# Moving the dummy matmuls at the start of a GEGLU kernel, and storing its last row tile in one piece

## The chip, the cores and the metric

One core of a Trainium2 chip runs the whole kernel. The metric is the device time of one execution in microseconds. A time is quoted as the median of several executions, with the lowest and highest. The profile of a kernel is one execution, recorded by the hardware; its span is about 1.8 us shorter than the device time.

## The reference, cut to what matters

```python
B, S, Dm, Df = 1, 2048, 1024, 3584            # x, w_gate, w_up, w_down in bf16
g = jnp.einsum("bsd,df->bsf", x, w_gate)
u = jnp.einsum("bsd,df->bsf", x, w_up)
h = jax.nn.gelu(g, approximate=True) * u
return jnp.einsum("bsf,fd->bsd", h, w_down)
```

## The kernel before

The matmuls of this kernel take `x` transposed, so its first 512 rows are transposed before the first of them. They come as four row tiles of 128 rows. Each is loaded, transposed by eight TensorE transposes into one PSUM bank, and copied to SBUF; row tile 1 is copied by ACT, the others by VectorE. In the profile TensorE starts a transpose every 0.107 us at first and every 0.056 us later, so its clock begins at about half rate; dummy matmuls on a constant tile ("dummies") run ahead of the transposes and between them, to bring the full clock sooner. In the profiles PE is TensorE, PEld its weight loads, DVE VectorE, ACT ScalarE; SPq and ACTq are the queues on which the sync engine and ACT issue loads and stores. A transfer lands when the profile shows it complete.

```python
def load_x(c):
    for i in range(NS):                                   # four row tiles, all on the sync queue
        nc.sync.dma_start(out=xn, in_=x2[r0 : r0 + P, :])

def turn(xT, xn, c, i):
    for ko in range(NKB):
        nc.tensor.transpose(tp[:, ko, :], xn[i][:, ko * P : (ko + 1) * P], ident)
    # ... the last tile's copy is cut in two
    (on_act if i == 1 else on_dve)(out=xT[c][:, ks, i * P : (i + 1) * P], in_=tp[:, ks])

# ...
keep_warm(NWARM, N)                                       # NWARM = 6 dummies of 512 columns
for i in range(NS):
    if i in (1, 2):
        keep_warm(5 - 2 * i, 2 * P)                       # 3, then 1 dummies of 256 columns
    turn(xT, xn0, 0, i)
plain(bank[0:4], 0, range(0, 2), parts=2)                 # first computing matmuls
```

`plain` begins with matmuls on the first 256 rows only (row tiles 0 and 1). Its first two matmuls need the first weights of `w_gate`, its third and fourth those of `w_up`; the ninth is the first that needs row tiles 2 and 3. At the end of the kernel the last row tile of the output leaves in two halves, on two queues:

```python
r0, h = (2 * ip + 1) * N + i * P, N // 2
for n, queue in enumerate((nc.sync, nc.scalar)):
    st = slot([P, h], bf16, "st")
    nc.scalar.copy(out=st, in_=e[i][:, n * h : (n + 1) * h])
    queue.dma_start(out=out2[r0 : r0 + P, n * h : (n + 1) * h], in_=st)
```

## Time and profile before

| | kernel before |
|---|---|
| time, median of 3 | 540.51 us (540.12 to 540.99) |
| span of the profiled run | 538.4 us |
| TensorE busy | 534.3 us, 99% |
| first and third computing matmul start | 7.23 and 7.45 us |
| end of the last matmul to the end of the span | 3.21 us |

Read the table from below: what is not TensorE's unbroken work is 7.2 us at the start and 3.2 us at the end, and the change is about those two stretches alone.

### The profile page before, as it was taken

To read this page: it belongs to the slowest core of one execution; us is meant where nothing else is said; L and a number is where in the kernel's file an instruction comes from. 1 tells how busy PE (TensorE), PEld (TensorE's weight loads), DVE (VectorE), ACT (ScalarE), POOL (GpSimd) and SP (SyncE) were. 2 spreads that over 40 slices of the span, in tenths; PEclk is the share of its full clock that TensorE was granted. 3 is DMA by queue.
4 is the path that set the end of the run, shared out by engine and by line. 5 is a ranking of instruction groups with operands and counts; after the bars stand their busy time and mean duration, and the time that the engine had idled before them with its cause. 6 is when DMAs were issued, how large, how long until landed. Compare 5 with 4: busy or idle time off the path is not lost.

```text
span 538.4 us, 7452 instructions
## 1 busy us (share of the span) xinstructions
PE 534.3 (99%) x2410; PEld 382.1 (71%) x2410; DVE 341.7 (63%) x524; ACT 261.4 (49%) x464; POOL 238.2 (44%) x215
## 2 busy tenths in 40 slices
PE   9999999999999999999999999999999999999997
PEld 5568686767767646888867677676868685488886
DVE  2986766767676895684955455555554649676730
ACT  2556675666666410255355555555555551114431
POOL 1079966777773500000097767676766600000000
PEclk9999999999999999999999999999999999999999
DMA  9765666749472999989872223241420049473751
GB/s 249 173 165 174 179 183 169 226 127 270 126 230 80 384 384 306 287 175 303 231 195 79 78 80 92 66 134 48 132 72 8 2 162 389 171 236 96 234 185 50
DMA packets 108326, 93.29 MB, mean 173 GB/s; under 512 B 17280, under 2 KB 93184, under 8 KB 108288
## 3 DMA queue, kind: packets, MB, share of 16 engines
q1 hardware_dynamic: 108144, 92.75, 59.2%
q8 instruction: 19, 0.31, 0.2%
q14 instruction: 19, 0.16, 0.1%
q10 hardware_dynamic: 144, 0.07, 0.0%
HBM read 74.45 MB, written 15.20 MB: 167 GB/s over the span
## 4 chain that ended last, share of the span: by engine, by line
PE 99%; DMA 1%; ACT 0%; issue 0%
PE bank L111 98%; PE bank L454 1%; DMA xn<-in_x_dram 1%; PE bank L509 0%; ACT st L418 0%
## 5 line engine op out<-in xcount | busy, mean ns | idle before, releaser
L93 POOL TENSOR_TENSOR s<-w 128x512 fp32r<-128x512 bf16 x102 | 119.1, 1190 | 162.8 <-PE bank L111 113.7
L111 PE MATMUL bank<-t,s 128*128 128x512 f32 x648 | 151.7, 390 | 0.0
L111 PEld LDWEIGHTS bank<-t,s 128*128 128x128 f32 x648 | 121.7, 188 | 25.5
L111 PE MATMUL bank<-xT,w 128*128 128x512 bf16 (+1 forms) x504 | 109.5, 376 | 0.0
L107 ACT COPY p<-bank 128x512 f32<-128x512 f32 x124 | 69.9, 590 | 45.3 <-PE bank L111 44.9
L111 PEld LDWEIGHTS <-w 128*128 128x128 bf16 x504 | 48.2, 98 | 57.8 <-issue 3.4
L90 DVE TENSOR_TENSOR hT<-g,bank 128x512 bf16<-128x512 f32 x112 | 76.8, 687 | 17.7 <-PE bank L111 4.5
L90 DVE TENSOR_TENSOR sum<-bank,p 128x512 f32<-128x512 f32 x54 | 37.3, 690 | 79.7 <-PE bank L111 78.6
L179 ACT ACTIVATE g<-sum 128x512 f32<-128x512 f32 x81 | 51.4, 635 | 74.6 <-DVE sum L90 74.3
L111 PE MATMUL bank<-q 128*128 128x512 f32 x240 | 59.0, 389 | 0.0
L93 POOL TENSOR_TENSOR s<-w,s 128x512 fp32r<-128x512 bf16 x50 | 57.8, 1179 | 0.0
L93 POOL TENSOR_TENSOR s<-s,w 128x512 fp32r<-128x512 f32 x50 | 57.3, 1168 | 0.0
L111 PE MATMUL bank<-t,sa 128*128 128x512 f32 x216 | 55.9, 401 | 0.0
L111 PE MATMUL bank<-tb,s 128*128 128x512 f32 x216 | 53.3, 389 | 0.0
L107 ACT COPY u<-bank 128x512 f32<-128x512 f32 x62 | 35.5, 589 | 33.5 <-PE bank L111 33.3
L111 PEld LDWEIGHTS bank<-q 128*128 128x128 f32 x240 | 45.1, 188 | 9.3
L111 PE MATMUL bank<-raw,hT 128*128 128x512 bf16 x224 | 48.7, 379 | 0.0
L102 ACT CAST tb<-raw 128x512 fp32r<-128x512 bf16 x28 | 17.3, 626 | 62.0 <-PE bank L111 26.7
L111 PEld LDWEIGHTS bank<-t,sa 128*128 128x128 f32 x216 | 40.6, 188 | 9.4
L111 PEld LDWEIGHTS bank<-tb,s 128*128 128x128 f32 x216 | 40.6, 188 | 8.4
L90 DVE TENSOR_TENSOR bank<-bank,p 128x512 f32<-128x512 f32 x54 | 37.7, 699 | 8.7 <-PE bank L111 6.2
L90 DVE TENSOR_TENSOR q<-hT 128x512 fp32r<-128x512 bf16 x56 | 38.4, 686 | 4.8 <-PE bank L111 4.8
(45 smaller groups left out, 443.8 us busy)
## 6 DMA issues: line engine op xcount, KB each, us to landing
raw<-in_w_down_dram SPq DMA_DIRECT2D x77, 256.0 KB, 5.1
q<-td SPq DMA_DIRECT2D x60, 256.0 KB, 5.2
w<-in_w_gate_dram SPq DMA_DIRECT2D x27, 512.0 KB, 5.9
w<-in_w_up_dram SPq DMA_DIRECT2D x27, 512.0 KB, 6.6
td<-m SPq DMA_DIRECT2D x12, 768.0 KB, 4.5
w<-td SPq DMA_DIRECT2D x6, 1024.0 KB, 9.5
out_dram<-st SPq DMA_DIRECT2D x31, 128.0 KB, 1.7
td<-w SPq DMA_DIRECT2D x2, 768.0 KB, 6.4
```

The lines of the kernel that those rows point to most:

```text
L90: nc.vector.tensor_tensor(out=out, in0=a, in1=b, op=op)
L93: nc.gpsimd.tensor_tensor(out=out, in0=a, in1=b, op=op)
L102: nc.scalar.copy(out=t, in_=src)
L107: nc.scalar.copy(out=t, in_=ps)
L111: nc.tensor.matmul(ps, lhsT=lhs, rhs=rhs, start=start, stop=stop, skip_group_check=True)
L179: nc.scalar.activation(g, src, ACT.Gelu_apprx_tanh)
L454: nc.tensor.transpose(tp[:, ko, :], xn[i][:, ko * P : (ko + 1) * P], ident)
```

## The change

Its intent: close the idle gap ahead of the first transpose with a seventh dummy, take away the dummies that delay row tile 1, and replace two small copies and two stores at the very end by one of each. A third edit drops an exception, so that in the last pass one more `w_down` tile is fetched as two halves.

```diff
-    NWARM = 6
+    NWARM = 7
...
-        for kh in (range(2),) if j < NJ - (1 if last else 2) else (range(1), range(1, 2)):
+        for kh in (range(2),) if j < NJ - 2 else (range(1), range(1, 2)):
...
         def put21(i):
-            if not last or i < NS - 1:
-                store(ip, 1, i, 0, lambda st: nc.scalar.copy(out=st, in_=e[i]))
-                return
-            r0, h = (2 * ip + 1) * N + i * P, N // 2
-            ...  (two copies, two stores, as above)
+            store(ip, 1, i, 0, lambda st: nc.scalar.copy(out=st, in_=e[i]))
...
-            if i in (1, 2):
-                keep_warm(5 - 2 * i, 2 * P)
+            if i == 2:
+                keep_warm(2, 2 * P)
```

## The prediction

> **What bounds the kernel now.** I read the page first (busy shares and the chain of waits by engine), then that chain in order of time, then the timeline of the first eight and the last seven microseconds, because the diff touches nothing else.
>
> ```profile
> PE 534.3 (99%) x2410; PEld 382.1 (71%) x2410; DVE 341.7 (63%) x524; ACT 261.4 (49%) x464; POOL 238.2 (44%) x215
> ...
> PE 99%; DMA 1%; ACT 0%; issue 0%
> ```
>
> TensorE is the bound over the whole span of 538.4 us; nothing else holds more than 1% of the chain. So a change can only gain where TensorE does not yet work, or does work that is not needed. The chain in order of time (start, length, what) shows where that is:
>
> ```profile
> 0.74 2.77 DMA xn<-in_x_dram
> 3.51 0.05 issue
> 3.56 1.04 PE bank L454 x8
> 4.59 0.64 PE bank L509 x3
> 5.24 0.85 PE bank L454 x8
> 6.09 0.21 PE bank L509
> 6.30 1.09 PE bank L454 x16
> 7.39 527.79 PE bank L111 x2368
> 535.18 0.02 issue
> 535.21 0.03 ACT st L418
> 535.23 0.24 issue
> 535.48 0.38 ACT st L418
> ```
>
> L454 are the transposes of the four row tiles, L509 the dummies between them, L111 every matmul that computes. The 2368 matmuls are one uninterrupted piece of 527.79 us that the diff does not enter. What can change is the 7.4 us ahead of it and the 3.2 us behind it (535.18 to 538.4). The timeline of the start:
>
> ```profile
> 2.01 0.15 PEld L509 LDWEIGHTS <-const-bfloat16-1.0 128*128 128x128 bf16 x1 [0.28 <-issue]
> 2.44 0.15 PEld L509 LDWEIGHTS <-const-bfloat16-1.0 128*128 128x128 bf16 x1 [0.28 <-issue]
> 3.56 0.77 PEld L454 LDWEIGHTS <-xn 128*128 128x128 bf16 x8 [0.97 <-DMA xn<-in_x_dram]
> 6.12 1.01 ACT L457 COPY xT<-bank 128x1024 bf16<-128x1024 bf16 x1 [4.11 <-PE bank L454]
> 7.23 17.45 PE L111 MATMUL bank<-xT,w 128*128 128x256 bf16 x88
> ```
>
> The weight loads of two dummies start 0.43 us apart, so a 512-column dummy takes 0.427 us. The sixth starts at 2.86 (timeline) and hands TensorE on at 2.86 + 0.43 = 3.29; the first transpose starts only at 3.56, when row tile 0 has landed. That **hole of 0.27 us** is the only idle time of TensorE at the start. The end:
>
> ```profile
> 532.04 0.58 ACT L413 CAST st<-bank 128x512 bf16<-128x512 f32 x1 [2.59 <-PE bank L111]
> 532.65 0.33 SPq L363 DMA_DIRECT2D out_dram<-st  x1
> 535.21 0.65 ACT L418 CAST st<-bank 128x256 bf16<-128x256 f32 x2 [2.59 <-PE bank L111]
> 535.61 0.33 SPq L419 DMA_DIRECT2D out_dram<-st  x1
> 535.89 0.37 ACTq L419 DMA_DIRECT2D out_dram<-st  x1
> ```
>
> The first two lines are the third row tile in one copy and one store, the form that the change gives to the last one; the other three are the last tile in halves.
>
> **What the Trainium skill says.** (1) TensorE: Matmul & The Clock Gate, Part 1: the array starts at half clock and goes to full after a window of about 3.4 us of activity; the window is free-running, so the moment varies by some 500 ns from run to run; a matmul of N columns issues every N/1.2 ns before and N/2.4 + 2.5 ns after. The trace agrees: 0.427 us for 512 columns early; transposes last 314 ns at first and 219 ns later. From 6.09 to 7.23 there are 16 transpose starts; n at 0.107 and 16 - n at 0.056 us make 1.14 for n near 5, so the full clock came at about 6.6 us. (2) The same page, Part 4, says that transposes do not count as activity in the same way. Here the clock came after 3.0 us that held 24 or more transposes and only 0.85 us of dummies, so the trace rather speaks against it; in any case both kernels issue the same dummy columns. (3) DMA: Bandwidth & Descriptors, "Anatomy of one DMA", puts most of the cost of a small transfer on a fixed receipt. That page describes another issuing path, but the trace agrees: a store of 128 KB lands 1.7 us after issue, those of 64 KB after 1.6 (sync queue) and 1.7 (ACT's queue). (4) ScalarE: Activation LUTs, "What ACT_TABLE_LOAD costs": 186 ns + 0.833 ns per column for one instruction without pointer operands. The trace's copies are a little shorter: 585 ns for 512 columns, 376 for 256.
>
> **The change part by part.** *Start.* Dummy columns before: 6x512 + 3x256 + 1x256 = 4096. After: 7x512 + 2x256 = 4096. Nothing is saved in work; dummies are moved into the hole. The landings, taken from the DMA view one issue at a time: the row tiles are issued at 0.74, 1.19, 1.65 and 2.12 and land after 2.8, 3.0, 3.8 and 4.2 us, thus at 3.5, 4.2, 5.4 and 6.3; the first weights of gate and up are issued at 2.59 and 3.07 and land after 4.2 and 4.1, thus at 6.8 and 7.2.
>
> With these landings and the clock at 6.6 as before, the changed start runs so: the seventh dummy ends at 2.86 + 2 x 0.427 = 3.71 (tile 0 is there since 3.5); tile 0 until 3.71 + 8 x 0.107 = 4.57 (tile 1 since 4.2); tile 1 until 5.42; two dummies of 0.213 until 5.85 (tile 2 since 5.4); then seven transposes at half clock until 6.60 and nine at 0.056 until 7.10 (tile 3, first needed at 6.65, since 6.3). The first real matmul starts at 7.10 instead of 7.23: **0.13 us earlier**. The check: 0.27 us of idle time at half clock is worth 0.135 us at full clock. The ACT copy of tile 1, which that matmul needs and which ended at 7.13, only just in time, now starts near 5.65 and ends near 6.7: that tight place is relieved. The up weights (7.2) are first needed by the third matmul at 7.10 + 0.22 = 7.32: still in time.
>
> *End.* Now: last matmul done 535.18; copies from 535.21 to 535.86; the second store is issued on ACT's queue at 535.89 and lands 1.67 later at 537.55, and 0.84 us of closing follow. After: one copy 535.21 + 0.585 = 535.79, store issued 0.03 later (535.82, as on the third tile: 532.62 to 532.65), lands 1.70 later at 537.52. **About 0.03 us earlier**, a tie: one copy is 0.07 us shorter than the overlapped pair, and the sync queue's 128 KB store is about 0.03 slower than the 64 KB store on ACT's.
>
> *A third thing in the diff:* in the last pass one more w_down tile, the last but one, is fetched as two halves. Its load is issued at 500.75 and lands at 504.33; VectorE's subtraction of it starts at 504.98, so the second half may come 0.6 us later without being felt. An issue takes 0.4 us. Cost: 0.
>
> *Sum:* 0.13 + 0.03 = 0.16 us for a run whose clock came at 6.6, out of 540.5: 0.03%.
>
> **The rivals.** *The start is bound by landings, not by TensorE.* If the clock is granted two microseconds earlier, both kernels wait for tiles 2 and 3 (5.4, 6.3) and for the up weights (7.2), and the start gains nothing. Taking the clock's moment as evenly spread over one window (0.78 + 3.4 to 7.6, an estimate from the skill's window and the first dummy), about two fifths of the runs have no gain, the rest 0.1 to 0.16: mean 0.08, so about 540.4. *The tighter arrivals cost:* the slack of tiles 1 to 3 falls from 0.85, 0.65, 0.5 to 0.4, 0.4, 0.35 us; row tiles landing 0.5 us later than in this trace would make tile 1 wait. Each 0.1 us beyond the slack costs 0.05 to 0.1; unlikely, since nothing moves the loads. *The closed hole changes when the clock comes:* an unbroken stretch may qualify a window that one with a hole misses. That would save half of a window at most, and the landings cut it to 0.5 us or so, in some runs only. *The split fetch stalls TensorE near 505 us:* VectorE is close behind there (three operations of 0.60 for each 1.81 us of TensorE), so a late half would show at once; the slack of 0.6 us speaks against it. Any of these stays below 0.6 us, a tenth of a per cent. A change of 2%, 10.8 us, would need a broken 527.79 us piece, and the order of instructions on all engines beyond start and end is the same.
>
> **Range and chances.** Mean start gain 0.08 to 0.13 and end gain 0.03 from 540.51: 540.51 - 0.15 = 540.36, say 540.35. The spread of the runs before (540.12 to 540.99, 0.87 us) is about what a wandering clock can do: a clock 1 us later costs 0.5 us. The range must hold that spread for a median of a few runs: 539.85 to 540.9. Faster by 2%: 0.003; slower by 2%: 0.003.
>
> **What would show it.** In the profile after: seven dummies 0.43 apart, then transposes with no wait for row tile 0 (before: 0.97 on the weight-load row) and none for tiles 1 to 3; the piece of real matmuls about 0.13 earlier, if the clock's step from 314 to 219 ns transposes is again near 6.6; one 0.58 us copy and one store of 1.7 us at the end; the long piece unchanged at 527.8. Wrong would be: a new wait for a row tile, a clock step in another window, a hole near 505 us, or a 128 KB store that lands later than 1.75 us after its issue.

## The result, and the profile after

| | before | after |
|---|---|---|
| time, median of 6 | 540.32 us (539.98 to 540.99) | 540.26 us (539.66 to 540.87) |
| span of the profiled run | 538.4 us | 538.8 us |
| first computing matmul | 7.23 us | 7.49 us |
| third computing matmul | 7.45 us | 7.91 us |
| end of the last matmul to the last landing | 2.38 us | 2.34 us |

The ratio is 0.9999, with a 95% interval of 0.9986 to 1.0012: no difference that can be seen. So the time is as predicted, but the one profile of the changed kernel is 0.4 us longer than that of the kernel before, against a predicted 0.16 us shorter. That needs an explanation. Its page first:

```profile
PE 534.1 (99%) x2409; PEld 381.2 (71%) x2409; DVE 341.5 (63%) x524; ACT 261.4 (49%) x463; POOL 238.5 (44%) x215
...
PE 98%; DMA 1%; SPq 0%; ACT 0%; issue 0%
```

One point of the chain's share has gone from TensorE to other things. The chain of waits in order of time (start, length, what) tells which; line numbers are 7 lower than before in this part of the kernel, so L447 are the transposes and L412 the last copy:

```profile
...
2.12 4.87 DMA xn<-in_x_dram
6.99 0.05 issue
7.04 0.62 PE bank L447 x8
7.66 0.22 PE bank L111 x2
7.88 0.03 issue
7.91 527.77 PE bank L111 x2366
535.68 0.02 issue
535.71 0.58 ACT st L412
```

The chain no longer runs back through TensorE's dummies but through a load: row tile 3, issued at 2.12, took 4.87 us to land. Then the chain holds the transposes of that tile, two matmuls, and a wait. The timeline of the start shows the same from TensorE's side; the bracket at the end of a line is idle time before it and what ended it:

```profile
0.78 3.15 PE L502 MATMUL bank<-const-bfloat16-1.0 128*128 128x512 bf16 x7 [0.78 <-PEq L640]
...
5.46 1.01 ACT L450 COPY xT<-bank 128x1024 bf16<-128x1024 bf16 x1 [3.45 <-PE bank L447]
...
6.30 0.45 PEld L447 LDWEIGHTS <-xn 128*128 128x128 bf16 x8 [0.94 <-DMA xn<-in_x_dram]
...
7.03 0.45 PEld L447 LDWEIGHTS <-xn 128*128 128x128 bf16 x8 [0.28 <-DMA xn<-in_x_dram]
...
7.91 1.10 PEld L111 LDWEIGHTS <-w 128*128 128x128 bf16 x11 [0.31 <-DMA w<-in_w_up_dram]
```

The seven dummies run without a gap into the transposes, as intended. But TensorE then waits three times: for row tile 2, for row tile 3, and for the first weights of `w_up`. None of these waits is in the kernel before's profile. The loads are issued at the same times in both (0.74, 1.19, 1.66, 2.12; up weights 3.07), yet row tile 2 landed at 6.26 instead of 5.45, tile 3 at 6.99 instead of 6.31, and the up weights at 7.87 instead of 7.17. The transposes also change from long to short at about 5.0 us, so the clock stepped up 1.6 us earlier than in the first profile. (The clock that the profile gives as granted reads 1.00 throughout; the step is read from these durations.) Everything behind the start is unchanged: the difference in start time between the two kernels' 2368 computing matmuls is 0.46 us at the third, 0.50 at the 200th and 0.50 at the last.

At the end, the DMA view of the changed kernel's last store (size, us from issue to landing):

```profile
out_dram<-st SPq DMA_DIRECT2D x1, 128.0 KB, 1.7
```

One copy of 0.58 us and one store that lands 1.7 us later: that half of the prediction is as written.

### The profile page after: what moved, and what is told of

Its sections match the earlier page's. It is cut to its first block, busy times and chain, and to the rows that moved or that the text cites. A ratio compares the mean times of both kernels' runs of the same rounds, so it can differ in the third digit from the quotient of the medians.

```text
span 538.8 us, 7447 instructions
## 1 busy us (share of the span) xinstructions
PE 534.1 (99%) x2409; PEld 381.2 (71%) x2409; DVE 341.5 (63%) x524; ACT 261.4 (49%) x463; POOL 238.5 (44%) x215
## 4 chain that ended last, share of the span: by engine, by line
PE 98%; DMA 1%; SPq 0%; ACT 0%; issue 0%
PE bank L111 98%; DMA xn<-in_x_dram 1%; SPq L440 0%; PE bank L447 0%; ACT st L412 0%
```

## The experiments

**Two theories.** *Clock theory*: the start is TensorE's own work at half clock, as the prediction's main sum has it, and the first profile after was an unlucky one. *Landing theory*: the start waits for loads in most runs, so moving dummies can gain nothing there. The noise came first, with the kernel before against itself, the changed kernel again, and each half of the change alone.

**aa_before** (no edit), timed in 5 rounds:

> The kernel before, unchanged, as the measure of noise and a second look at its start. Both theories: ratio to itself 1.000, with an interval of about 0.1% either way, so that a gain of 0.1 to 0.16 us (0.03%) cannot be read from the time. Landing theory (the start is set by when row tiles 2 and 3 and the first up weights land, in most runs): the third computing matmul starts within 0.1 us of the latest of the landings, and that moment differs from the first profile's 7.45 us by some tenths of a us because the landings differ. Clock theory (the start is set by TensorE's own work at half clock): it starts at 7.45 plus half of the shift of the clock's step from 6.6 us.

Measured: 540.16 us (539.88 to 540.25), the kernel before beside it 540.38 (539.91 to 540.75, 9 runs), ratio 0.9996 with an interval of 0.9982 to 1.0009. So a kernel differs from itself by as much as the change was to gain. The profile brought something that neither theory had. Its chain in order of time:

```profile
...
5.30 0.72 PE bank L454 x8
6.02 0.02 issue
6.04 1.02 ACT xT L457
7.06 0.04 issue
7.11 527.95 PE bank L111 x2368
```

The clock stepped at about 5.7 us here, TensorE was done with its transposes before 6.9, the up weights had landed at 6.98, and the first matmul waited for **ACT's copy of row tile 1**, which ended at 7.05. There is a third thing that can hold the start, and both expectations missed: the third matmul came at 7.32, against 7.08 at the latest by landings (6.98 + 0.1) and 7.0 by the clock.

**after_again** (the changed kernel, no edit), 5 rounds:

> The changed kernel again. Landing theory: same time as before within the noise, and in its profile a wait of TensorE for a row tile or for the first weights whenever the clock's step comes before about 5.8 us. Clock theory: a clock step near or after 6.6 us and no wait for a landing, with the third computing matmul about 0.13 us earlier than the kernel before would have it. Both: seven dummies, no wait for row tile 0; end of the last matmul to landing of the last store about 2.34 us (2.38 before).

Measured: 540.17 us (539.50 to 540.69), ratio 0.9996, interval 0.9983 to 1.0008: the same as aa_before had against itself. Its profile is again bound by landings although the clock stepped at about 5.8: row tile 2 at 6.29, up weights at 7.91, third matmul at 7.96. Last matmul to last landing: 2.34 us.

**start_only** and **end_only**: one half of the change each.

```diff
 # start_only, from the kernel before
-    NWARM = 6
+    NWARM = 7
-            if i in (1, 2):
-                keep_warm(5 - 2 * i, 2 * P)
+            if i == 2:
+                keep_warm(2, 2 * P)
```

```diff
 # end_only, from the changed kernel
-    NWARM = 7
+    NWARM = 6
-            if i == 2:
-                keep_warm(2, 2 * P)
+            if i in (1, 2):
+                keep_warm(5 - 2 * i, 2 * P)
```

> The changed start with the old end. End: from the end of the last matmul to the landing of the last store 2.38 us as in the kernel before, with two copies of 0.37 and two stores. Start: as in the changed kernel, no hole ahead of the first transpose (below 0.05 us of idle TensorE); a later wait for row tile 2 or 3 if the landings of those are again near 6.3 and 7.0 us (landing theory), none if near 5.4 and 6.3 and the clock steps at 6.6 (clock theory).

> The old start with the changed end. End: one copy of 0.585 us, one store, 2.34 us from the end of the last matmul to the landing. Start: a hole of about 0.27 us ahead of the first transpose; landing theory: a wait for tile 2 or 3 or for the weights here too if the clock steps early, so that the hole costs nothing; clock theory: none.

Measured, one look each: 540.01 and 540.03 us. The ends are what the edits say: 2.38 us from the last matmul to the last landing with two stores, 2.34 with one. Both starts waited for the up weights (landed at 7.21 and 7.24; third matmul at 7.25 and 7.29). In end_only the gap ahead of the first transpose was 0.2 us and cost nothing, because TensorE stood waiting for tiles 2 and 3 and for the weights later anyway.

**no_dummies** takes all dummies away and **eleven_ahead** puts eleven in front and none between, to see how much TensorE's own work can grow or shrink before the start feels it.

```diff
 # from the changed kernel
-    NWARM = 7
+    NWARM = 0                       # eleven_ahead: 11
-            if i == 2:
-                keep_warm(2, 2 * P)
```

> The changed kernel without any dummy: the transposes are TensorE's first work, at about 3.56 us. If transposes count as activity, the clock steps up one window of 3.4 us after they began at the earliest, so between about 7.0 and 10.4 us, and every us that computing matmuls run before it costs 0.5 us: between 0 and 1.5 us more, about 541.0 us. If transposes do not count (as the Trainium skill says, TensorE: Matmul & The Clock Gate, Part 4), the window has to be filled by computing matmuls alone, so the step comes at about 10.8 to 14.2 us and costs 1.7 to 3.4 us, about 542.7. Landing theory of the start: the first computing matmul is not later than in the changed kernel by more than the 8 slow transposes of tile 3 cost (0.4 us), because it waits for landings anyway. If the place of dummies were all that matters to the start (clock theory in its strict form), the whole 1.5 us would show.

> Eleven dummies ahead of the first transposes, none between. TensorE comes to tile 0 at about 5.4 us (0.78 + 0.38 + 10 x 0.427, less if the clock steps up before) instead of 3.7. Landing theory: tiles 0 to 2 are there by then or nearly, no wait for them, and the start of the third computing matmul moves by 0.4 us at most against the landing of the up weights. Clock theory: 2048 - 512 = 1536 more dummy columns (11x512 against 7x512 + 2x256) cost 0.64 us at full clock up to 1.28 at half.

no_dummies measured 540.82 us (540.52 to 541.44, 4 runs), ratio 1.0013, interval 0.9999 to 1.0027: about 0.7 us longer, and near the 541.0 expected if transposes count as activity rather than the 542.7 if they don't. Its profile, first the group of transposes (min/median/max duration in ns), then two pieces of its chain:

```profile
L447 PE MATMUL bank<-ident,xn x32: 286/311/314, 3.3 to 7.2; 128*128 128x128 bf16 x32
```

```profile
5.61 1.89 PE bank L447 x16
7.49 528.04 PE bank L111 x2368
```

All 32 transposes ran at the long, half-clock duration, and the fourth computing matmul, at 7.9 us, was the first at full clock. By then TensorE had run nothing but transposes since 3.26 us and three matmuls since 7.29. A window of 3.4 us (the Trainium skill's, Part 1 of the page named) that ends at 7.9 begins at 4.5 and is filled by transposes but for one wait of 0.34 us (for row tile 2) and the first matmuls. Could those 0.6 us of matmuls have done it alone? In the kernel before, 2.5 us of dummies (0.78 to 3.29) had not: the step came at 6.6. So transposes do count, at least in part. And all dummies together are worth some 0.7 us (the interval reaches from nothing to 1.5). That a better place for them is worth less than this is likely, but no run shows it.

eleven_ahead measured 541.58 us in one look, its third matmul at 7.93 us. Both theories had this wrong in form: the up weights had landed at 7.17, and TensorE's transposes were issued by 7.29. What held the start was ACT's copy again, from 6.65 to 7.67, because eleven dummies push row tile 1 back. (Another 0.9 us of this run was lost at 205 to 208 us, 0.6 of it in two waits of TensorE for loads of `w_down`; swap_copies below lost 0.3 us at the same place, none of the other twelve profiles anything. Why is not shown; swap_copies has the seven and two dummies of the changed kernel.)

**The revised theory: three bounds.** The third computing matmul starts when the latest of three things is done: the loads have landed (row tile 3 plus its transposes, first weights), TensorE has got through dummies and transposes at the clock it happens to have, and ACT has copied row tile 1 (1.01 us after that tile's transposes). Two more experiments move the landings out of the way.

**two_queues** issues row tiles 1 and 3 on ACT's queue, so that the weights behind them are issued about 0.95 us earlier. **both_ends** adds a last copy in two halves on two engines.

```diff
 # two_queues, from the changed kernel
-            nc.sync.dma_start(out=xn, in_=x2[r0 : r0 + P, :])
+            queue = (nc.sync, nc.scalar)[i % 2]
+            got = queue.dma_start(out=xn, in_=x2[r0 : r0 + P, :])
+            if queue is not nc.sync:
+                tc.keep_in_program_order(got)
 # both_ends, in addition, for the last row tile
+                nc.scalar.copy(out=st[:, : N // 2], in_=e[i][:, : N // 2])
+                nc.vector.tensor_copy(out=st[:, N // 2 :], in_=e[i][:, N // 2 :])
```

> The changed kernel with row tiles 1 and 3 issued on ACT's queue, so that the first weights are issued at about 1.65 us instead of 2.60. Landing theory: the first up weights land earlier than the 7.2 to 7.9 us of the traces so far, by up to 0.9 us if the issue binds and by about 0.3 if the DMA engines do (their busy share is near 100% from 2.5 us on), and the computing matmuls begin as much earlier, until TensorE's own work or ACT's copy of tile 1 binds. In the time: -0.3 us, at the edge of what can be read. Clock theory: no change unless the clock steps early.

> As two_queues, and the last row tile copied in two halves at the same time, one by ACT and one by VectorE, into one tile with one store. End: the copies end 0.38 us after they start instead of 0.585, so last matmul to last landing 2.14 us instead of 2.34, if VectorE's half takes no longer than ACT's 0.38. Start as two_queues. Together 0.2 to 0.6 us less than the kernel before, about 540.0; the ratio's interval of 0.13% either way may not show it, the profile will.

two_queues measured 539.84 us (539.66 to 540.29), the kernel before beside it 540.11, ratio 0.9995, interval 0.9983 to 1.0008. In its profile the up weights landed at 6.60 instead of 6.98 to 7.91 in the profiles so far, and the start moved on to the next bound, ACT's copy of row tile 1, which ends at 5.62 + 1.01 = 6.63:

```profile
5.62 1.01 ACT L453 COPY xT<-bank 128x1024 bf16<-128x1024 bf16 x1 [2.67 <-PE bank L450]
...
6.68 1.03 PE L111 MATMUL bank<-xT,w 128*128 128x256 bf16 x8
```

That is the earliest start of all profiles (third matmul 6.90). It has a price: row tile 0 landed at 3.96, against 3.31 to 3.58 in the eight profiles with one queue and the kernel's own dummies, so the gap ahead of the first transpose is back, with 0.3 us (3.71 to 4.01). both_ends measured 539.83 us (539.64 to 540.70), ratio 0.9994, interval 0.9980 to 1.0008; its profile fell on a late clock step (6.7 us), and TensorE's own work held the start (first matmul 7.33). Its end failed. The timeline:

```profile
535.34 0.37 ACT L413 CAST st<-bank 128x256 bf16<-128x256 f32 x1 [2.59 <-PE bank L111]
535.74 0.42 DVE L414 CAST st<-bank 128x256 bf16<-128x256 f32 x1 [11.29 <-ACT st L413]
536.19 0.33 SPq L363 DMA_DIRECT2D out_dram<-st  x1
```

VectorE's half waits for ACT's, as the bracket says, so the copies take 0.83 us instead of 0.585 and the last landing comes 2.58 us after the last matmul instead of 2.34. The Trainium skill, PSUM — Partial Sum Buffer, "Terms", says that two engines must not access one PSUM bank, in the same quarter of its partitions, at once, reads against reads included. Both halves read one bank on all 128 partitions, and the wait keeps them apart; the expectation had overlooked it. Whether the wait comes from the bank or from the shared SBUF tile no run shows. A compilation without a chip speaks for the bank: with two separate SBUF tiles the program still makes VectorE's copy wait for ACT's.

**two_queues_old_dummies**: the kernel before with the same early loads, to see what the place of the dummies is worth once landings do not hide it.

```diff
 # from the kernel before: the loads of two_queues, nothing else
-            nc.sync.dma_start(out=xn, in_=x2[r0 : r0 + P, :])
+            queue = (nc.sync, nc.scalar)[i % 2]
+            ...
```

> The kernel before (old dummies, old end) with the row tiles on two queues, which made the landings early (tiles 4.0, 4.2, 5.6 and 5.8 us, up weights 6.6). With the landings out of the way the place of the dummies should show. Three-bound theory (the start is the latest of landings, TensorE's own work at the clock it has, and ACT's copy of row tile 1): three dummies now delay tile 1 and with it ACT's 1.01 us copy, so the first computing matmul starts at about 7.03 us for a clock step at 5.1, 7.33 at 5.7, 7.67 at 6.7, 0.33 later than the new dummies would give at the same step (6.70, 6.99, 7.34); mean over the steps 0.31 us later than two_queues, so about 540.2 us, and TensorE waits for ACT's copy in the profile. If the place of the dummies did not matter at all: as two_queues.

Measured: 539.80 us (539.64 to 540.73), ratio 1.0000 to the kernel before beside it, interval 0.9986 to 1.0013; two_queues had 0.9995. The difference of 0.0005 is 0.27 us, in the expected direction and near the expected 0.31, but the intervals overlap widely, and of the two medians this one is the lower, so the time does not show it. The chain of its profile does show the expected wait:

```profile
5.68 1.02 ACT xT L460
...
6.74 527.96 PE bank L111 x2368
```

The clock stepped at 4.5 us here. Between the starts for steps at 4.3 and 5.1 us (6.65 by the same reckoning, worked out afterwards, and 7.03), 6.74 is where it should be, and TensorE waited for ACT's copy although the transposes were issued by 6.42.

**swap_copies**: two_queues with VectorE copying row tile 1 and ACT row tile 2.

```diff
-            (on_act if i == 1 else on_dve)(out=xT[c][:, ks, i * P : (i + 1) * P], in_=tp[:, ks])
+            (on_act if i == 2 else on_dve)(out=xT[c][:, ks, i * P : (i + 1) * P], in_=tp[:, ks])
```

> two_queues with row tile 1 copied by VectorE (0.69 us) and row tile 2 by ACT (1.01) instead of the other way round. Three-bound theory: ACT's copy of tile 1 held the start in two_queues (6.64 us, first matmul 6.68); now the first matmul waits for TensorE's own transposes or for VectorE's copy, about 6.53 us with a clock step at 5.1; with a late step (6.7) no gain (7.33). Mean gain 0.05 to 0.15 us, not readable in time. Risk: the ninth matmul needs tile 2's copy, which ends about 7.3 us; it starts 0.87 us after the first, so a short wait is possible.

Measured: 539.76 us (539.38 to 540.66), ratio 0.9995, interval 0.9982 to 1.0007. The clock stepped at about 6.35 us, late, and the start (7.15) was TensorE's own work, so this profile does not test the swap. This is the fastest median of all, but no interval leaves 1.000 out: **no version that beats both kernels was shown.** The nearest to it is what the four versions with early loads have in common: their 20 runs average 540.00 us, the 18 runs of the kernel before beside them 540.19, a difference of -0.19 with an uncertainty of 0.21.

**before_look** and **after_look** (no edits): one more profile of each start.

> One more look at the start of the kernel before. Three-bound theory: the first or third computing matmul starts within 0.06 us of the latest of: landing of the first up weights + 0.045, end of ACT's copy of tile 1 + 0.05, end of the last transpose's issue. With a clock step before 5.6 us: landings or ACT's copy; later: TensorE or ACT's copy.

> One more look at the start of the changed kernel. Three-bound theory as for before_look, but ACT's copy of tile 1 ends at least 0.4 us before the first computing matmul (it starts before 5.7 us), so it never binds: landings if the clock steps before about 6.3 us, TensorE's own work after. If tile 2 again lands near 6.3 us instead of 5.3 to 5.6 as in the other traces, the start is bound by landings whatever the clock does.

They measured 540.12 and 540.30 us, and their third matmuls came 0.05 us after the up weights, as forecast. Here are all eight profiles with the row tiles on one queue, in us. "Clock" is where transposes, or the dummies among them, turn from long to short (in end_only all transposes were short, so 3.5 is the latest that it can be), "copy" the end of ACT's copy of tile 1; the last column is what the third matmul, or the first, waited for.

| profile | dummies | clock | tile 2, tile 3 land | up weights land | copy | 1st, 3rd matmul | held by |
|---|---|---|---|---|---|---|---|
| before | old | 6.6 | 5.45, 6.31 | 7.17 | 7.14 | 7.23, 7.45 | TensorE |
| aa_before | old | 5.7 | 5.33, 6.13 | 6.98 | 7.05 | 7.11, 7.32 | ACT's copy |
| before_look | old | 4.3 | 5.66, 6.47 | 7.29 | 6.24 | 6.97, 7.34 | landing |
| end_only | old | 3.5 | 5.54, 6.44 | 7.24 | 5.96 | 6.94, 7.29 | landing |
| after | new | 5.0 | 6.26, 6.99 | 7.87 | 6.48 | 7.49, 7.91 | landing |
| after_again | new | 5.8 | 6.29, 7.00 | 7.91 | 6.67 | 7.51, 7.96 | landing |
| after_look | new | 4.9 | 5.93, 6.61 | 7.52 | 6.41 | 7.12, 7.57 | landing |
| start_only | new | 5.0 | 5.59, 6.33 | 7.21 | 6.44 | 6.83, 7.25 | landing |

In the six landing rows the third matmul follows the up weights by 0.04 to 0.05 us. In all eight the span is the start of the third matmul plus 530.9 us (530.90 to 530.97), so this one moment is all of the difference between them but 0.07 us. In that rest the ends can be told apart: 530.93 to 530.97 with two stores, 530.90 to 530.93 with one. The three bounds hold in every row, and the copy of tile 1 never binds with the new dummies in these four.

**What stays open.** In three of the four profiles with the new dummies row tile 2 landed later (5.93 to 6.29) than in any with the old (5.33 to 5.66). start_only has the same start and landed at 5.59, no_dummies and eleven_ahead at 5.56 and 5.07. In after and after_again the packet records hold one or two 2 KB packets that took 1.5 us, where the median is 0.08 us; no run tells why. Eight profiles cannot say whether that is chance, but the spans of the timed runs help. If nothing is lost in the middle, the third matmul starts 530.9 us before the end of the span (an estimate from the table's profiles). By the spans that is at 6.8 to 8.1 us in the 12 runs of the changed kernel, and at 7.2 to 8.1 in 33 of the kernel before. A span of 538.6 us or more, a third matmul at about 7.7 or later, came in 3 of the 12 and in 6 of the 33. So starts as late as those of after and after_again also happen with the old dummies, though none of their four profiles caught one, and these two profiles are of the slowest quarter of their kernel's runs. The timed runs also speak against a lasting cost: over everything timed, the mean of 12 runs of the changed kernel is 540.24 us and of 39 of the kernel before 540.25, with a spread (standard deviation) of 0.40 and 0.27, so the difference of the means is -0.01 with an uncertainty of about 0.25. A gain of 0.1 us, none, and a loss of 0.2 all fit.

## Why the prediction was right or wrong, point by point

- **What bounds the kernel, and that only 10 us can change.** Right: the 2368 computing matmuls keep their spacing, and time and range came out as written (540.26 us inside 539.85 to 540.9). That hit does not bear out the mechanism of the start: the interval of the ratio reaches from 0.76 us less to 0.65 us more, and holds a gain of 0.16 us, none, and a loss alike.
- **Start, 0.13 us earlier.** The steps up to 4.57 us held to 0.01 us in the profile after: seventh dummy, tile 0 with no wait, tile 1 with no wait. The step that failed, in every profile of the new start, is the one called "With these landings and the clock at 6.6 as before". Both are properties of a run, not of the kernel. The clock stepped at 4.9 to 5.8 us in the profiles of the new start, and tile 2 landed at 5.59 to 6.29 instead of 5.4. So tile 2 did not start at 5.85 but at 6.31 in the profile after, and the start was 0.26 us later at the first matmul and 0.46 at the third, not 0.13 earlier.
- **"Unlikely, since nothing moves the loads."** Wrong: nothing in the program moves them, but landings of unchanged loads differ by up to 1 us between executions (up weights 6.98 to 7.91). The slack of 0.4 us that the prediction worked out was smaller than that spread.
- **The rival "the start is bound by landings".** This was the right account, mis-sized: the prediction gave it two fifths of the runs; it held the start in all four profiles of the new dummies and in two of four of the old. Two terms were off: the range of the clock's step, put at 4.2 to 7.6 us, where end_only had it at 3.5, and the landings, taken as fixed.
- **ACT's copy of tile 1, "only just in time", is relieved.** Right: with one queue and the new dummies it ended 0.8 to 1.4 us ahead of the third matmul. The prediction treated it as a side remark; it is a bound of its own, which held the start in aa_before, two_queues, two_queues_old_dummies and eleven_ahead. What the relief is worth in time is not shown.
- **The closed hole changes the clock.** Not shown either way: the step wandered from 3.5 to 6.6 us with the old dummies and from 4.9 to 5.8 with the new.
- **End, 0.03 us earlier.** Right: 2.38 to 2.34 us from last matmul to last landing, and end_only against start_only shows it as the edit's own doing. It is read from the profiles; no time shows it.
- **The split fetch costs nothing.** Right: the second half landed at 504.64 and VectorE's subtraction started at 505.48, 0.8 us later, without a mark on TensorE.
- **Transposes count as activity.** The prediction leaned to it; no_dummies showed it. Its reading of the first profile was off in the count: 21 transposes start between 3.56 and 6.6 us, not 24 or more.

## What to carry to other kernels

In a start of a few microseconds, look at several profiles before sizing a gain: here the landings wandered by one microsecond and the clock's step by three, and the start is the latest of several chains, so shortening one of them pays only in the runs where it is last. List the chains (loads, TensorE's own work, the copy behind the transposes), and move the one that is last most often. Closing an idle gap ahead of a wait for a load that comes last moves the gap, not the end.

## What the Trainium skill lacked or had wrong

- TensorE: Matmul & The Clock Gate, Part 4, has it that transposes do not count as TensorE activity for the clock in the same way. In no_dummies the full clock came at 7.9 us, with nothing but transposes since 3.26 us and three matmuls ahead of it; and in end_only all 32 transposes ran at the full clock (218 to 230 ns).
- The same page, Part 1, asks for a window of about 3.4 us of sustained work before the full clock. In end_only the transposes already ran short at 3.5 us, 2.7 us after TensorE's first recorded instruction, so less work than that was enough. The page's spread of 500 ns either way is too small for this start: with the old dummies the step came between 3.5 and 6.6 us.
- No page gives the spread of a load's landing from run to run; DMA: Bandwidth & Descriptors, "Latency and other measured facts", names 0.2 us of access latency on average and 2 us under high load. For the same load of 128 KB, issued at 3.07 us in all eight profiles with one queue, the landing came between 6.98 and 7.91 us.
